# A decode block with its gradients: the first weight in longer rows, all slots in one tile, and one weight load cut by rows

## The chip, the cores and the metric

The kernel runs on one core of a Trainium2 chip. The metric is the device time of one execution in microseconds (us), as a median over runs.

## The reference

```python
def block(x, k_cache, v_cache, wq, wo, w1, w3, w2):      # cut from the reference
    q = (layernorm(x) @ wq)            # x: 4 x 1 x 512, wq: 512 x 4096, 32 heads of 128
    p = softmax(q . k_cache * Dh**-0.5)                  # k_cache, v_cache: 4 x 32 x 4096 x 128, bf16
    h = x + (p . v_cache) @ wo                           # wo: 4096 x 512
    return h + (silu(layernorm(h) @ w1) * (layernorm(h) @ w3)) @ w2    # w1, w3: 512 x 1792, w2: 1792 x 512

out, vjp = jax.vjp(block, x, k_cache, v_cache, wq, wo, w1, w3, w2)
return out, *vjp(grad_out)
```

There are 128 pairs of batch and head. Each has 1 MB of K and 1 MB of V to read, V is read a second time for the gradients, and 1 MB each of K's and V's gradient is written. The arithmetic per byte is small.

## The kernel before

On-chip memory is cut into 23 slots of 128 partitions x 8320 bytes, which are handed round by hand. K and V heads come in as 128 rows of 8192 bytes, one row to a partition, in the first half all on the sync engine's queue. The parts that the change touches (cuts marked):

```python
class Slot:
    def __init__(self, name, src=free):
        self.i = src.popleft()
        self.t = slotp.tile([P, SLOT], BF16, name=name, tag=f"slot{self.i}")   # one tile per slot
# ... cut
wq_s = [Slot(f"wq{cc}") for cc in range(DC)]
for cc in range(DC):                                     # first weight: 4 loads of 128 rows x 8192 bytes
    nc.sync.dma_start(out=wq_s[cc].b(HD), in_=A_wq[cc * P:(cc + 1) * P, :])
# ... cut: K loads follow, as far as slots are free
for h in range(H):
    for cc in range(DC):
        nc.tensor.matmul(qT_ps[:, h, :], lhsT=wq_s[cc].b(HD)[:, h * Dh:(h + 1) * Dh], rhs=xhatT[:, cc, :],
                         start=(cc == 0), stop=(cc == DC - 1))
# ... cut
def load_w2():                                           # down projection: 2 loads of 128 rows x 7168 bytes
    sl = two_slots("w2")
    for i in range(2):
        nc.sync.dma_start(out=sl[i].b(7 * D).rearrange("p (c j) -> p c j", c=7),
                          in_=B_w2.rearrange("(p c) j -> p c j", c=FC)[:, i * 7:(i + 1) * 7, :])
    return sl

def d_hh_units():                                        # w2 transposed, times grad_out: early in the first half
    w2 = load_w2()
    # ... cut
```

The first half (to about 700 us) streams K and V through scores, softmax and the V product. The second (from about 740 us) reads V again and writes both cache gradients.

## Time and profile before

| what | before | where it stands |
|---|---|---|
| time, median of 3 | 1722.01 us (1721.88 to 1723.07) | the runs |
| span of the profiled run | 1720.0 us | first line of the page |
| bytes moved | 707.86 MB, mean 412 GB/s | packet line |
| rate in 20 to 660 us | 411 to 419 GB/s at a DMA share of 1.01 | busy times by stretch |
| busiest compute engine | TensorE, 77% | busy times |

The DMA share says what part of the time the sixteen DMA engines had a packet in hand. GB/s says what they moved. A share of 1.01 says that they had one in hand all the time.

One more view is needed that is not on the page. The trace keeps each DMA packet's start, duration and size, and for each transfer the sixteen times at which its parts, one to a DMA engine, signalled completion. "Packets took ..." and "lag" below are read from these records; the lag of a transfer is the time from its first to its last part.

### The profile page before, as it was taken

The numbers are of one execution on the slowest core, as the hardware profiler recorded it, in microseconds if no ns is written. First come the engines' busy times: TensorE is split into PE (matmuls) and PEld (weight loads), VectorE is DVE, ScalarE is ACT, GpSimd is POOL, SyncE is SP. The second block draws the span as 40 slices with busy tenths as digits, with TensorE's granted clock in tenths as the row PEclk, the third lists the DMA queues.
The fourth block names the chain that finished last, engine by engine and source line by source line (L and its number), as shares of the span: only waits on it lengthen the run. The fifth ranks groups of instructions, "written<-read, shape, count | busy, mean of one in ns | idle before, by whom it ended". The sixth has DMA issues, their size and how long they took to land. (4 is left out here: it accounts for less than half of the span.)

```text
span 1720.0 us, 44172 instructions
## 1 busy us (share of the span) xinstructions
PE 1331.8 (77%) x19124; PEld 1131.8 (66%) x19124; DVE 1253.1 (73%) x1389; ACT 960.3 (56%) x1470; POOL 414.4 (24%) x689
## 2 busy tenths in 40 slices
PE   5889888888888888888788787883677778677852
PEld 4767766766667666877677777773565566555652
DVE  5989899899998997667676776763567557456575
ACT  3455444444454444677655555553676667676752
POOL 1211222222222231231322222321223122212220
PEclk8999999999999999666655555555875565565556
DMA  9999999999999999999999999999999999999996
GB/s 397 418 419 419 419 418 420 418 419 418 412 418 405 418 402 395 380 424 424 424 424 425 424 425 425 424 425 398 411 388 410 422 421 417 404 420 419 419 421 273
DMA packets 101762, 707.86 MB, mean 412 GB/s; under 512 B 11052, under 2 KB 15288, under 8 KB 17600
## 3 DMA queue, kind: packets, MB, share of 16 engines
q1 hardware_dynamic: 63568, 432.04, 60.9%
q0 software_dynamic: 20864, 148.22, 20.6%
q10 hardware_dynamic: 17136, 124.79, 17.7%
q8 instruction: 150, 2.46, 0.5%
q14 instruction: 44, 0.36, 0.1%
HBM read 422.59 MB, written 282.34 MB: 410 GB/s over the span
## 5 line engine op out<-in xcount | busy, mean ns | idle before, releaser
L761 ACT COPY V<-pt_tps 128x1024 bf16<-128x1024 bf16 x512 | 492.5, 1016 | 200.4 <-PE pt_tps L760 175.2
L760 PE MATMUL pt_tps<-ident_b,V 128*128 128x128 bf16 x4096 | 454.1, 293 | 82.9 <-ACT V L761 78.6
L760 PEld LDWEIGHTS <-V 128*128 128x128 bf16 x4096 | 402.7, 138 | 146.2 <-issue 137.1
L766 DVE TENSOR_TENSOR gv<-P,reps 128x4096 bf16<-128x4096 bf16 x125 | 287.2, 2297 | 195.8 <-ACT reps L1129 92.4
L766 DVE TENSOR_TENSOR gk<-dS,reps 128x4096 bf16<-128x4096 bf16 x128 | 294.0, 2297 | 113.5 <-DMA out_dram<-gv 90.8
L433 PE MATMUL M_ps<-PK,Vn 128*128 128x130 bf16 x4096 | 287.4, 223 | 46.4 <-DMA Vn<-in_A_v_cache_dram 44.3
L418 DVE TENSOR_TENSOR PK<-Kn,PK 128x4096 bf16<-128x4096 bf16 x128 | 292.3, 2284 | 31.7 <-POOL PK L414 31.4
L433 PEld LDWEIGHTS <-Vn 128*128 128x128 bf16 x4096 | 254.9, 100 | 67.1 <-DMA Vn<-in_A_v_cache_dram 59.2
L325 DVE STREAM_TRANSPOSE KT<-Kn 128x512 f32<-128x512 f32 (+1 forms) x321 | 250.6, 797 | 0.3 <-issue 0.2
L320 ACT COPY KT<-pt_tps 128x1024 bf16<-128x1024 bf16 x128 | 129.5, 1012 | 192.9 <-PE pt_tps L319 145.7
L777 POOL DMA_DIRECT2D out_dram<-gv x128 | 68.4, 534 | 673.2 <-DVE dSt L1158 581.9
L1148 PE MATMUL dP_ps<-dOT_bf,V 128*128 128x1 bf16 x4096 | 149.9, 166 | 83.4 <-ACT V L761 58.7
L1148 PEld LDWEIGHTS <-V 128*128 128x128 bf16 x4096 | 140.1, 103 | 96.8 <-ACT V L761 70.2
L1138 POOL COPY P<-P_all 128x64 bf16<-128x64 bf16 x125 | 157.8, 1263 | 0.0
L331 POOL TENSOR_TENSOR W<-qrep,wmask 128x128 bf16<-128x128 bf16 x128 | 123.6, 966 | 82.7 <-PE S_ps L351 67.8
L414 POOL COPY PK<-P_all 128x64 bf16<-128x64 bf16 x128 | 32.6, 255 | 421.4 <-ACT P_all L408 418.4
L408 ACT COPY P_all<-pt_P 32x64 bf16<-32x64 bf16 x256 | 52.1, 203 | 58.9 <-PE pt_P L404 56.7
L1129 ACT CAST reps<-rep_ps 128x512 bf16<-128x512 f32 x62 | 36.4, 587 | 83.8 <-PE rep_ps L1126 46.5
L319 PE MATMUL pt_tps<-ident_b,Kn 128*128 128x128 bf16 x1024 | 81.2, 224 | 0.0
L319 PEld LDWEIGHTS <-Kn 128*128 128x128 bf16 x1024 | 62.6, 100 | 25.8 <-issue 25.8
L443 PE MATMUL kP_ps<-PK,onesw 128*32 128x512 bf16 x1024 | 79.4, 387 | 0.0
L351 PE MATMUL S_ps<-KT,W 128*32 128x256 bf16 x1536 | 75.2, 285 | 0.5 <-DVE KT L325 0.2
(239 smaller groups left out, 1284.9 us busy)
## 6 DMA issues: line engine op xcount, KB each, us to landing
Kn<-in_A_k_cache_dram SPq DMA_DIRECT2D x128, 1024.0 KB, 15.7
Vn<-in_A_v_cache_dram SPq DMA_DIRECT2D x128, 1024.0 KB, 16.1
out_dram<-gv POOLq DMA_DIRECT2D x128, 1024.0 KB, 29.0
out_dram<-gk SPq DMA_DIRECT2D x128, 1024.0 KB, 22.7
V<-in_A_v_cache_dram ACTq DMA_DIRECT2D x119, 1024.0 KB, 15.1
V<-in_A_v_cache_dram SPq DMA_DIRECT2D x9, 1024.0 KB, 18.7
wq<-in_A_wq_dram SPq DMA_DIRECT2D x8, 1024.0 KB, 19.0
out_dram<-gw POOLq DMA_DIRECT2D x6, 896.0 KB, 38.3
```

Of the source, the lines that this page charges most:

```text
L319: nc.tensor.transpose(pt[:, i, :], Kn[:, c * GW + i, :], ident_b[:])
L320: nc.scalar.copy(out=KT[:, c * GW:(c + 1) * GW, :], in_=pt[:])
L325: nc.vector.transpose(out=KT[:, c * w_:(c + n) * w_], in_=Kn[:, c * w_:(c + n) * w_])
L331: nc.gpsimd.tensor_tensor(out=W[:, hl], in0=qrep[:, :, s:s + 1].to_broadcast([P, 4, 32]), in1=wmask[:, hl, None, :].to_broadcast([P, 4, 32 ...
L418: nc.vector.tensor_tensor(out=PK[:, :, 0:Dh].rearrange("p j (r t) -> p j r t", t=2), in0=Ks[s].heads().rearrange("p j (r t) -> p j r t", t=2),
L433: nc.tensor.matmul(hold["M"][:], lhsT=Vn[:, j, :], rhs=PK[:, j, :], start=(j == 0), stop=(j == SJ - 1))
L443: nc.tensor.matmul(hold["kP"][32 * q:32 * (q + 1), :, :], lhsT=ones_window(w), rhs=PK[:, j0:j0 + 4, 0:Dh], start=(w == 0 and c == 0), stop ...
L760: nc.tensor.transpose(pt[:, i, :], v[:, g * GW + i, :], ident_b[:])
L761: nc.scalar.copy(out=v[:, g * GW:(g + 1) * GW, :], in_=pt[:])
L766: nc.vector.tensor_tensor(out=dst.rearrange("p j (r t) -> p j r t", t=2), in0=col2[:, :, None, :].to_broadcast([P, SJ, Dh // 2, 2]), in1=r ...
L1138: nc.gpsimd.tensor_copy(out=P2s[s][:], in_=P_all[:, s, :, None].to_broadcast([P, SJ, 2]))
L1148: nc.tensor.matmul(dP_ps[:, j:j + 1], lhsT=VT[:, j, :], rhs=dOT_bf[:, s:s + 1], start=True, stop=True)
```

## The change

Its intent is threefold: to load the first weight in 16384-byte rows, two loads in place of four; to make every slot a slice of one tile, so that two neighbouring slots can take one such load; and to shift load off one DMA engine by cutting the down projection's weight, in the first half only, into 120 and 8 rows. The author's estimate of that shift: the cut spares one engine 16 rows of 7168 bytes and gives eight others two rows more each. At the 269 ns at which such rows start one after the other before, this is 16 x 269 ns = 4.3 us less on the one and 0.54 us more on each of the eight.

```diff
+    arena = slotp.tile([P, NSLOT * SLOT], BF16, name="arena")
     class Slot:
-            self.t = slotp.tile([P, SLOT], BF16, name=name, tag=f"slot{self.i}")
+            self.t = arena[:, self.i * SLOT:(self.i + 1) * SLOT]
 ... cut
-    for cc in range(DC):
-        nc.sync.dma_start(out=wq_s[cc].b(HD), in_=A_wq[cc * P:(cc + 1) * P, :])
+    wq_v = []
+    for a in range(0, DC, 2):
+        v = arena[:, wq_s[a].i * SLOT:wq_s[a].i * SLOT + 2 * HD].rearrange("p (c n) -> p c n", c=2)
+        nc.sync.dma_start(out=v, in_=A_wq[a * P:(a + 2) * P, :].rearrange("(p c) n -> p c n", c=2))
+        wq_v += [v[:, 0], v[:, 1]]
 ... cut: rows_to_T reads the activations with a stride of two, the q matmuls read wq_v[cc]
-    def load_w2():
+    def load_w2(cuts=(0, P)):
         sl = two_slots("w2")
         for i in range(2):
-            nc.sync.dma_start(out=sl[i].b(7 * D).rearrange("p (c j) -> p c j", c=7),
-                              in_=B_w2.rearrange("(p c) j -> p c j", c=FC)[:, i * 7:(i + 1) * 7, :])
+            for lo, hi in zip(cuts, cuts[1:]):
+                nc.sync.dma_start(out=sl[i].b(7 * D).rearrange("p (c j) -> p c j", c=7)[lo:hi],
+                                  in_=B_w2.rearrange("(p c) j -> p c j", c=FC)[lo:hi, i * 7:(i + 1) * 7, :])
 ... cut
     def d_hh_units():
-        w2 = load_w2()
+        w2 = load_w2((0, 120, P))
```

More of the change, by code (lines that the diff above doesn't have):

```diff
@@ L220, in rows_to_T @@
         pt = psA.tile([P, nchunks, n], FP32, tag="rT", name="pt_rT")
+        rows = src_rows.rearrange("b (a p c) -> b a c p", c=2, p=P)
         for c in range(nchunks):
-            nc.tensor.transpose(pt[:, c, :], src_rows[0:n, c * P:(c + 1) * P], ident_f[0:n, 0:n])
+            nc.tensor.transpose(pt[:, c, :], rows[0:n, c // 2, c % 2, :], ident_f[0:n, 0:n])
         nc.vector.tensor_copy(out=dst, in_=pt[:])
@@ L271 @@
             for cc in range(DC):
-                nc.tensor.matmul(qT_ps[:, h, :], lhsT=wq_s[cc].b(HD)[:, h * Dh:(h + 1) * Dh], rhs=xhatT[:, cc, :],
+                nc.tensor.matmul(qT_ps[:, h, :], lhsT=wq_v[cc][:, h * Dh:(h + 1) * Dh], rhs=xhatT[:, cc, :],
                                  start=(cc == 0), stop=(cc == DC - 1))
```

## The prediction

> **What bounds the kernel now.** I read the page's slices first, then the busy times by stretch, the first weight's own view, the last stretch, and last how the change moves instructions and waits on each engine.
>
> ```profile
> span 1720.0 us, 44172 instructions
> PE 1331.8 (77%) x19124; PEld 1131.8 (66%) x19124; DVE 1253.1 (73%) x1389; ACT 960.3 (56%) x1470; POOL 414.4 (24%) x689
> ...
> DMA  9999999999999999999999999999999999999996
> GB/s 397 418 419 419 419 418 420 418 419 418 412 418 405 418 402 395 380 424 424 424 424 425 424 425 425 424 425 398 411 388 410 422 421 417 404 420 419 419 421 273
> DMA packets 101762, 707.86 MB, mean 412 GB/s; under 512 B 11052, under 2 KB 15288, under 8 KB 17600
> ```
>
> No compute engine is above 77%, while the DMA row is full in 39 slices of 40 and the rate stands at 418 to 425 GB/s in most of them. 707.86 MB at 420 GB/s would be 1685 us: all but 35 us of the span is the transfer of bytes that the change leaves as they are. The stretches say where the 35 us are:
>
> ```profile
> 0.00:20.00 20.00, 7.26 (x165) 6.47 (x166) 6.36 (x24) 2.41 (x4) 3.86 (x21) 1.00 0.92 371
> 20.00:240.00 220.00, 187.44 (x3032) 153.00 (x3032) 196.44 (x268) 114.88 (x242) 50.72 (x131) 0.95 1.01 419
> 240.00:460.00 220.00, 185.71 (x3079) 151.93 (x3076) 202.33 (x267) 107.09 (x243) 57.15 (x128) 0.99 1.01 418
> 460.00:660.00 200.00, 166.27 (x2772) 137.90 (x2772) 182.28 (x243) 96.98 (x217) 54.96 (x119) 0.99 1.01 411
> 660.00:740.00 80.00, 70.12 (x1121) 60.50 (x1121) 51.07 (x77) 46.67 (x69) 16.07 (x21) 0.79 1.00 385
> 740.00:1190.00 450.00, 347.71 (x4376) 322.59 (x4374) 301.95 (x254) 256.94 (x284) 119.23 (x130) 0.56 1.01 425
> 1190.00:1320.00 130.00, 94.04 (x1340) 81.74 (x1341) 80.21 (x74) 87.85 (x102) 30.66 (x32) 0.74 0.98 394
> 1320.00:1690.00 370.00, 271.79 (x3216) 216.53 (x3214) 223.07 (x183) 245.77 (x313) 81.20 (x109) 0.58 1.01 418
> 1690.00:1720.00 30.00, 1.42 (x39) 1.16 (x35) 9.45 (x8) 1.69 (x2) 0.53 (x1) 0.55 0.51 211
> ```
>
> The last two columns are the DMA share and GB/s. From 20 to 660 us the share is 1.01[...]: no engine of the 16 lacks work. What is lost is lost in the first 20 us, around 660 to 740 and 1190 to 1320, and in the last 30. Of these the change touches only the first. Its weight:
>
> ```profile
> L132 SPq DMA_DIRECT2D wq<-in_A_wq_dram x4: 388/422/956, 0.7 to 2.1; - x4
> its engine sat idle before it (us, times) until:
>   DMA wq<-in_A_wq_dram: 7.1, 4
> ...
> DMA to landing us min/median/max: 5.3/8.4/11.4
> ```
>
> TensorE waits 7.1 us for the four loads and starts its last 125 matmuls at 13.57 us, but the DMA engines meanwhile fetch K and V, so this wait costs time only if they later run dry, and they do not before 460 us. The last stretch has a different cause:
>
> ```profile
> 1700.00:1705.00 5.00, 0.00 (x0) 0.00 (x0) 0.00 (x0) 0.00 (x0) 0.00 (x0) 0.50 0.87 362
> 1705.00:1710.00 5.00, 0.00 (x0) 0.00 (x0) 0.00 (x0) 0.00 (x0) 0.00 (x0) 0.50 0.07 31
> 1710.00:1715.00 5.00, 0.00 (x0) 0.00 (x0) 0.00 (x0) 0.00 (x0) 0.00 (x0) 0.50 0.07 28
> ```
>
> A share of 0.07 is one DMA engine of sixteen: one straggler works alone for some 12 us. The sixteen landing times of each transfer, which the trace holds, agree: fifteen parts of the last store are in by 1701.2 us, the sixteenth at 1717.5. The same landings give the lag between the first and the last engine earlier: 0.75 us after the first weight, 3.0 at 100 us, 9.3 at 450, 5.2 at 690. In the first half this lag is not one engine's. Eight of the sixteen each lose about 1.5 us in turn, at the times when a 16384-byte instruction fetch runs (150 of them, one per 10 us), and at 450 us these eight lie together, between 9.0 and 9.3 us behind.
>
> [...]
>
> **The change part by part.** First weight. A packet of 8192 bytes is recorded with 309 ns, one of 7168 with 272 and one of 3584 with 140 (medians); starts on one engine follow each other 3 ns sooner than these. 132 ns for 3584 bytes are 36.8 ns per KB, so 8192 bytes cost 295 of 306 ns and about 11 ns are the fixed part. Four loads of 128 rows are 32 packets on each engine; two loads of 16384-byte rows are 16. Saved: 16 x 11 = 0.18 us per engine, and two completion writes of about 6 ns. Sum: -0.19 us, an estimate. It is on the path as far as the engines are, from the first microsecond on.
>
> Wait order at the start. The sync engine keeps eight transfers in flight; with two loads fewer ahead, K runs two loads further forward (10 MB instead of 8 MB queued). With a share of 1.01 a deeper queue moves nothing: 0.
>
> Order of contraction. The rows are now interleaved in pairs, and the transposed activations are read with a stride of two; four small transposes (0.58 us together, at 8.9 us) and 128 matmuls of 166 ns in number, size and order as before: 0.
>
> Down projection's weight in the first half (about 60 us; the second load, at the end, stays uncut). [...] The sum over engines is zero, so the mean rate stays; only the lag changes. Two more issues on the sync queue (about 0.33 us each) cancel the two saved.
>
> One tile for all slots. Every engine keeps its instructions, shapes and order, apart from one small row that moves by a place. The waits change in few places: 65 of 1388 on VectorE, mostly a wait for ScalarE traded for another that has long been met; 2 of TensorE's go away with the two loads. One long wait goes: three small GpSimd copies that in before sat 26.4 us until 701 us for a V load now wait for GpSimd alone. Their reader, the first gradient product, starts at 706.0 us because of the row copied just before it, so the 26.4 us gain nothing: 0.
>
> Sum: -0.2 us, plus whatever the shifted lag does, between 0 and +0.5 us by the rivals below. 1722.0 - 0.2 + a little is 1721.9; I choose 1721.6, a little lower, because a tuner keeps a change rather when it gains.
>
> **The rivals.** First: [...] relieving it by 4.3 us brings the last K, V and weights in earlier, so that the phase ends up to 4 us sooner: 1718. For it: the author chose the cut, and from 460 us on the rate falls to 411[...]. Against it: at 450 us eight engines lie within 0.3 us of each other, so taking one out leaves seven in the same place.
>
> Second: [...] Then the last landing of the phase comes 0.5 us later: 1722.3. [...]
>
> Third: the new dependences of the one tile order something that ran freely, and a store or load of the second half is issued later. [...] a few microseconds, either way: 1718 to 1726. Against it: the waits compared above, which are nearly all met long before.
>
> Fourth: the first half ends sooner and the gain is swallowed at 700 to 740, where all engines drain (the lag falls to 0.4 us at 725 us) and the second half starts from a chain of small steps. Then even a correct gain of the first rival shows only in part.
>
> **Range and chances.** The three runs of before lie within 1.2 us. Mechanisms bring -4 to +0.5 us, a shifted schedule perhaps 2 us more: 1718.0 to 1724.5 for 8 in 10. Two per cent are 34 us. That is as much as all the time in which the engines are below their rate, so neither a gain nor a loss of that size has a source here: faster 0.01, same 0.98, slower 0.01.
>
> **What would show each step right or wrong.** First weight: its loads land together near 13.4 us, and packets of 16384 bytes take about 600 ns each, not less. The cut: after the 60 us mark the landings have one engine 4.3 us ahead of where it was, while the largest lag at 100 and 450 us stays at 3.0 and 9.3 (or 0.5 more if the second rival holds); if it falls by over 1 us, the first rival is right. Queue: share and GB/s of 20 to 660 us unchanged. One tile: GpSimd's wait of 26.4 us gone, the first gradient product still near 706 us. End: still a share of 0.07 for about 12 us, as the change does not touch the last stores. The prediction would be wrong if the tail's straggler vanished or grew by more than 5 us, or if VectorE or the sync queue showed a new wait of tens of microseconds.

## The result, and the profile after

| | before | after |
|---|---|---|
| time, median of 4 | 1722.41 us (1721.88 to 1723.07) | 1729.01 us (1727.73 to 1730.08) |
| ratio after to before | | 1.0038 (95%: 1.0020 to 1.0055) |
| span and clock of the profiled run | 1720.0 us, 0.749 | 1728.3 us, 0.761 |

Ratios here are the mean time of one kernel's fast runs over that of the other's in the same rounds, so not quite the ratio of the medians quoted. The change makes the kernel 6.6 us slower: "same" at the 2% mark, but outside the predicted range of 1718.0 to 1724.5.

Three lines of the page after: span, DMA share and rate in 40 slices of 43 us.

```profile
span 1728.3 us, 44122 instructions
...
DMA  9999999999999999999999999999999999999996
GB/s 397 366 418 418 419 418 419 417 416 418 414 414 411 418 403 391 378 422 423 424 425 424 425 425 425 424 425 402 394 393 405 425 419 415 404 418 422 420 421 271
```

The share is as full as before. Slice two of the rate, 43 to 86 us, reads 366 where before has 418; every other slice lies within 6 of its counterpart but one (394 for 411, near 1220 us). (418 - 366) x 43.2 us = 2.2 MB not moved, or 5.4 us at 418 GB/s. The same in two of the wide stretches that the prediction shows of before (columns: busy us and counts of TensorE, its weight loads, VectorE, ScalarE, GpSimd; granted clock, DMA share, GB/s):

```profile
20.00:240.00 220.00, 183.97 (x2947) 148.54 (x2946) 191.58 (x261) 113.31 (x236) 47.36 (x127) 0.95 1.01 408
240.00:460.00 220.00, 187.29 (x3080) 153.86 (x3080) 201.35 (x268) 105.64 (x241) 58.62 (x132) 0.98 1.01 417
```

408 against 419 GB/s in the first, at the same share of 1.01; 417 against 418 in the second. Within slice two, in steps of 4 us, before:

```profile
60.00:64.00 4.00, 4.00 (x80) 3.24 (x80) 3.82 (x4) 1.08 (x5) 1.57 (x2) 1.00 1.03 424
64.00:68.00 4.00, 2.81 (x38) 2.16 (x37) 3.75 (x11) 2.20 (x5) 1.11 (x5) 1.00 1.00 412
68.00:72.00 4.00, 3.33 (x56) 2.79 (x60) 3.33 (x3) 2.68 (x7) 0.24 (x1) 1.00 1.01 420
```

and after:

```profile
60.00:64.00 4.00, 3.79 (x78) 3.23 (x79) 3.83 (x3) 1.23 (x6) 1.27 (x2) 1.00 1.03 238
64.00:68.00 4.00, 3.12 (x43) 2.29 (x40) 3.69 (x9) 1.90 (x5) 1.39 (x5) 1.00 1.04 241
68.00:72.00 4.00, 0.04 (x1) 0.00 (x0) 3.61 (x4) 1.89 (x2) 0.00 (x0) 0.76 0.96 224
72.00:76.00 4.00, 0.94 (x9) 0.94 (x10) 0.00 (x0) 0.00 (x0) 0.00 (x0) 0.50 1.00 414
```

For 12 us all sixteen engines are busy (0.96 to 1.04) and move 224 to 241 GB/s instead of 412 to 424. Step by step that is 4 x (424 - 238)/424 + 4 x (412 - 241)/412 + 4 x (420 - 224)/420 = 5.3 us of transfer lost. It is the time in which the down projection's weight comes in: its 256 packets of 7168 bytes took 486 ns on average (median 480) where before they took 277 (274), and the 8192-byte packets of K and V sent between them took 570 ns against 313. At the end of the stretch TensorE runs dry, as its timeline after shows (start, duration, engine, work, in brackets the idle time before and what ended it):

```profile
75.06 2.51 PEld L438 LDWEIGHTS <-arena 128*128 128x128 bf16 x24 [7.10 <-DMA arena<-in_A_v_cache_dram]
```

It sat 7.10 us for a V load queued behind the slow one. How far the same VectorE instruction of the two traces is shifted tells when time was lost: 0.4 us until 67.8 us, 7.7 to 8.2 us from 72 to 100, 5.6 from 118 to 174, 4.4 to 7.1 until 660, 5.2 to 6.6 from 700 to 732, 5.7 to 7.6 from 750 to 1170, and 8.1 at the end of these two runs. The loss of 5.3 us in those 12 us is there at once, and it stays. The 1 to 3 us that come on top after 740 us are of these two profiled runs, and no run here explains them; the medians differ by 6.6 us.

The first weight's loads after, by their line (issue times, then from issue to landing), and the matmuls behind them:

```profile
L135 SPq DMA_DIRECT2D arena<-in_A_wq_dram x2: 392/406/421, 0.7 to 1.2; - x2
...
DMA to landing us min/median/max: 12.8/12.8/12.8
```

```profile
14.08 3.52 PE L277 MATMUL qT_ps<-xhatT,arena 128*128 128x4 bf16 x126 [3.23 <-DMA arena<-in_A_wq_dram]
```

They start at 14.08 us instead of 13.57. The end, in steps of 5 us after:

```profile
1713.30:1718.30 5.00, 0.00 (x0) 0.00 (x0) 0.00 (x0) 0.00 (x0) 0.00 (x0) 0.50 0.06 26
1718.30:1723.30 5.00, 0.00 (x0) 0.00 (x0) 0.00 (x0) 0.00 (x0) 0.00 (x0) 0.50 0.07 28
```

is what it was: one engine of sixteen, alone for about 12 us, only later.

### The profile page after: what moved, and what is told of

It reads as the page before. It is cut to its first block, busy times and chain, and to the rows that moved or that the text cites. A ratio compares the mean times of both kernels' runs of the same rounds, so it can differ in the third digit from the quotient of the medians.

```text
span 1728.3 us, 44122 instructions
## 1 busy us (share of the span) xinstructions
PE 1322.2 (77%) x19124; PEld 1122.8 (65%) x19124; DVE 1252.8 (72%) x1389; ACT 959.2 (56%) x1470; POOL 414.0 (24%) x689
## 3 DMA queue, kind: packets, MB, share of 16 engines
q0 software_dynamic: 20864, 148.22, 20.5%
## 5 line engine op out<-in xcount | busy, mean ns | idle before, releaser
L767 ACT COPY arena<-pt_tps 128x1024 bf16<-128x1024 bf16 x512 | 491.9, 1017 | 201.2 <-PE pt_tps L766 179.3
L766 PE MATMUL pt_tps<-ident_b,arena 128*128 128x128 bf16 x4096 | 445.6, 289 | 89.7 <-ACT arena L767 84.2
L766 PEld LDWEIGHTS <-arena 128*128 128x128 bf16 x4096 | 395.1, 136 | 153.4 <-issue 144.5
L772 DVE TENSOR_TENSOR arena<-P,arena 128x4096 bf16<-128x4096 bf16 x125 | 287.2, 2297 | 195.7 <-DMA out_dram<-arena 102.7
L772 DVE TENSOR_TENSOR arena<-dS,arena 128x4096 bf16<-128x4096 bf16 x128 | 294.0, 2297 | 113.3 <-DMA out_dram<-arena 101.0
L438 PE MATMUL M_ps<-arena 128*128 128x130 bf16 x4096 | 287.5, 223 | 64.9 <-DMA arena<-in_A_v_cache_dram 64.4
L423 DVE TENSOR_TENSOR arena<-arena 128x4096 bf16<-128x4096 bf16 x128 | 292.4, 2285 | 37.0 <-POOL arena L419 36.3
L438 PEld LDWEIGHTS <-arena 128*128 128x128 bf16 x4096 | 253.6, 99 | 86.9 <-DMA arena<-in_A_v_cache_dram 80.6
L330 DVE STREAM_TRANSPOSE arena<-arena 128x512 f32<-128x512 f32 (+1 forms) x321 | 250.5, 797 | 0.0
L325 ACT COPY arena<-pt_tps 128x1024 bf16<-128x1024 bf16 x128 | 129.4, 1012 | 196.0 <-PE pt_tps L324 153.1
L1154 PE MATMUL dP_ps<-dOT_bf,arena 128*128 128x1 bf16 x4096 | 149.8, 166 | 86.8 <-ACT arena L767 59.9
L1154 PEld LDWEIGHTS <-arena 128*128 128x128 bf16 x4096 | 139.0, 103 | 100.5 <-ACT arena L767 71.6
L324 PE MATMUL pt_tps<-ident_b,arena 128*128 128x128 bf16 x1024 | 80.2, 223 | 0.0
L448 PE MATMUL kP_ps<-arena,onesw 128*32 128x512 bf16 x1024 | 79.9, 389 | 0.0
L324 PEld LDWEIGHTS <-arena 128*128 128x128 bf16 x1024 | 61.7, 99 | 25.7 <-issue 25.6
```

Source lines behind the costliest of these rows:

```text
L324: nc.tensor.transpose(pt[:, i, :], Kn[:, c * GW + i, :], ident_b[:])
L325: nc.scalar.copy(out=KT[:, c * GW:(c + 1) * GW, :], in_=pt[:])
L330: nc.vector.transpose(out=KT[:, c * w_:(c + n) * w_], in_=Kn[:, c * w_:(c + n) * w_])
L423: nc.vector.tensor_tensor(out=PK[:, :, 0:Dh].rearrange("p j (r t) -> p j r t", t=2), in0=Ks[s].heads().rearrange("p j (r t) -> p j r t", t=2),
L438: nc.tensor.matmul(hold["M"][:], lhsT=Vn[:, j, :], rhs=PK[:, j, :], start=(j == 0), stop=(j == SJ - 1))
L448: nc.tensor.matmul(hold["kP"][32 * q:32 * (q + 1), :, :], lhsT=ones_window(w), rhs=PK[:, j0:j0 + 4, 0:Dh], start=(w == 0 and c == 0), stop ...
```

## The experiments

The theory after reading the two traces: the cut slows the packets themselves, its own (486 ns for 277) and those sent between them (570 for 313), because its pieces have fewer than 128 rows, with a price of its own for each shape. What in the shape would do that, no record of this case shows; the runs can ask only which shapes are slow.

The rivals: (A) it is the long rows or the one tile, not the cut; (B) it is the number of transfers or their smaller size; (C) any shape other than 128 rows is slow for itself, at one price for all of them; and the prediction's own first rival, that the relief of one engine matters.

### First round: which part, and is it rows or pieces

Four kernels, run on one chip beside seven runs of before (median 1721.86 us, 1721.41 to 1723.06).

**e1_no_cut**: the kernel after, with the weight uncut.

```diff
-        w2 = load_w2((0, 120, P))
+        w2 = load_w2()
```

> The whole change, but the down projection's weight in two loads of 128 rows again. All three theories that lay the loss on the cut ([...] fifteen: fifteen engines instead of sixteen; transfers: four transfers instead of two) expect the loss of 6.6 us to go almost whole: 1722.0 to 1723.5 us, and 418 GB/s again between 60 and 72 us. The theory that the one tile or the 16384-byte rows cost the time expects 1727 to 1729.

Measured 1723.57 us (1721.16 to 1725.18), ratio 1.0008 (0.9993 to 1.0023). The packets of 7168 bytes took 277 ns again, and the rate is back:

```profile
60.00:64.00 4.00, 3.94 (x80) 3.20 (x78) 3.84 (x4) 1.10 (x6) 1.63 (x2) 1.00 1.03 424
```

Rival A falls.

**e2_cut_only**: the kernel before, with the cut and nothing else.

```diff
-        w2 = load_w2()
+        w2 = load_w2((0, 120, P))       # load_w2 as in the change
```

> The kernel before, and only the cut into 120 and 8 rows. Theories of the cut: 1727 to 1729 us, with the packets of 7168 bytes at some 480 ns instead of 272. Theory of the one tile or the first weight: 1722 to 1723.

Measured 1728.64 us (1727.52 to 1729.47), ratio 1.0038 (1.0023 to 1.0053): the whole loss of the change, by the cut alone. The packets took 524 ns (median 522).

```profile
60.00:64.00 4.00, 4.00 (x80) 3.27 (x80) 3.81 (x4) 1.08 (x5) 1.56 (x2) 1.00 1.06 236
```

**e3_columns**: as many transfers, but each of 128 rows; the cut goes through the columns (4 and 3 of 7).

```diff
-                nc.sync.dma_start(out=sl[i].b(7 * D).rearrange("p (c j) -> p c j", c=7)[lo:hi],
-                                  in_=B_w2.rearrange("(p c) j -> p c j", c=FC)[lo:hi, i * 7:(i + 1) * 7, :])
+                nc.sync.dma_start(out=sl[i].b(7 * D).rearrange("p (c j) -> p c j", c=7)[:, lo:hi],
+                                  in_=B_w2.rearrange("(p c) j -> p c j", c=FC)[:, i * 7 + lo:i * 7 + hi, :])
-        w2 = load_w2((0, 120, P))
+        w2 = load_w2((0, 4, 7))
```

> The whole change, with the weight still in four transfers, but each of all 128 rows: columns are split (4096 and 3072 bytes a row). [...] Fifteen: no loss either. Transfers (four of them hold four of the eight places in the queue): still 1727 to 1729.

Measured 1722.64 us (1722.05 to 1723.53), ratio 1.0004 (0.9989 to 1.0019). Packets of 4096 bytes took 163 ns, of 3072 bytes 124 ns: 287 for what was 277 in one.

```profile
60.00:64.00 4.00, 3.60 (x75) 2.85 (x72) 3.80 (x4) 1.44 (x6) 1.97 (x4) 1.00 1.02 405
```

Rival B falls: four transfers cost nothing measurable, if each spans all rows.

**e4_64_64**: the cut in two equal halves, so that the sixteen engines have equal work and none is relieved (in e9 all sixteen signals of a 64-row load come with the data).

```diff
-        w2 = load_w2((0, 120, P))
+        w2 = load_w2((0, 64, P))
```

> The whole change, with the weight cut into 64 and 64 rows. Sixteen engines with four rows each, all the same work. [...] Fifteen: no loss, 1722 to 1723.5, since all sixteen engines work equally.

Measured 1729.03 us (1725.93 to 1731.52), ratio 1.0035 (1.0018 to 1.0051); packets took 576 ns (median 539).

```profile
60.00:64.00 4.00, 3.88 (x79) 3.32 (x80) 3.82 (x3) 1.15 (x6) 1.36 (x2) 1.00 1.01 158
```

An even split over all engines costs as much as the uneven one, so the loss is not an imbalance of work among engines. That leaves the shape of the pieces, with a price for each shape or with one price for all (rival C).

### Second round: size of the effect, the tail, and a miss

Four kernels beside seven runs of before (median 1722.59 us, 1720.33 to 1724.34).

**e5_one_tile**: the kernel before, with the slots as slices of one tile and nothing else.

```diff
+    arena = slotp.tile([P, NSLOT * SLOT], BF16, name="arena")
-            self.t = slotp.tile([P, SLOT], BF16, name=name, tag=f"slot{self.i}")
+            self.t = arena[:, self.i * SLOT:(self.i + 1) * SLOT]
```

> Only the one tile for all slots; the first weight in four loads and the down projection's weight in two, as before. If the cut is the whole loss, as the first four runs say: 1721.5 to 1723.5, same as before within 0.1%. If the one tile costs something that the first four runs hid behind the first weight's gain: above 1724.

Measured 1722.78 us (1720.57 to 1723.28), ratio 0.9997 (0.9982 to 1.0012). The one tile costs and brings nothing that can be seen.

**e6_k_120_8**: the same cut on other data, K's loads of heads 16 to 31, in the kernel before. If the cut itself is the cause, 16 MB must lose far more than 1.8 MB.

```diff
-            nc.sync.dma_start(out=Ks[s].heads(), in_=cache_head(A_k_cache, s))
+            cuts = (0, 120, P) if 16 <= s < 32 else (0, P)
+            for lo, hi in zip(cuts, cuts[1:]):
+                nc.sync.dma_start(out=Ks[s].heads()[lo:hi], in_=cache_head(A_k_cache, s)[lo:hi])
```

> The kernel before with sixteen of the 128 K loads (heads 16 to 31) cut into 120 and 8 rows: the cost of the cut many times over. [...] the cut weight (1.84 MB) cost 5 to 6 us, so sixteen loads of 1.05 MB each cost 46 to 52 us if all of it stays exposed[...]: 1755 to 1775 us. A theory that the loss came once, from a hole in the queue at that place, expects under 1735.

Measured 1789.59 us (1785.39 to 1794.18), ratio 1.0388 (1.0362 to 1.0413): 67 us slower, more than expected.

```profile
80.00:240.00 160.00, 99.51 (x1361) 83.02 (x1358) 82.86 (x112) 51.88 (x106) 15.10 (x54) 0.82 1.00 242
```

Share 1.00, 242 GB/s: against the 419 of before, 160 us x (1 - 242/419) = 67.6 us, the whole difference. The count seems to have left out that V's loads in the same queue, of 128 rows as ever, are slowed too: in steps of 20 us from 80 to 220 us, 8192-byte packets of both together took 479 to 596 ns on average (315 before), and if only K's half had doubled to 612 the mean would be about 460. What passes the delay on to loads of 128 rows, no run shows by itself.

**e7_112_16**: the cut at 112 rows. Both pieces have parts on all sixteen engines: in e9, for 112 rows and for 16, all sixteen signals come with the data.

```diff
-        w2 = load_w2()
+        w2 = load_w2((0, 112, P))
```

> The kernel before with the weight cut into 112 and 16 rows. Both parts use all sixteen engines, with seven rows and one. [...] A theory that any shape other than 128 rows is slow for itself expects about 500 ns and 1727 to 1729 again.

Measured 1727.03 us (1726.37 to 1729.38), ratio 1.0026 (1.0011 to 1.0041), packets 504 ns (median 492). The author's own estimate was lower than that of rival C and did not hold.

```profile
60.00:64.00 4.00, 3.79 (x78) 3.06 (x75) 3.82 (x4) 1.25 (x6) 1.79 (x2) 1.00 1.04 212
```

504 ns and 1727.03 us are what rival C expects: about 500 ns, 1727 to 1729 us. But packets here run among those of K and V; what a shape costs by itself had to be tested without the stream: e9 below.

**e8_gv_sync**: a look at the tail and its straggler. V's gradient stores, which before has on GpSimd and so on the software queue (q0 of its page, 148.22 MB), go out through the sync engine.

```diff
-        nc.gpsimd.dma_start(out=rows_of(out_3[b, h]), in_=gv.heads())
+        nc.sync.dma_start(out=rows_of(out_3[b, h]), in_=gv.heads())
```

> Not a test of the cut but of its aim. The kernel before with the V gradient's stores issued by the sync engine instead of GpSimd. If the one engine that works alone for the last 12 us is slow because of the software queue, its lag goes and the end comes up to 12 us earlier: 1708 to 1716. If it is slow for another reason: 1720 to 1726. If the sync engine's eight places in flight are too few for loads and all stores: slower, 1730 or more.

Measured 1724.23 us (1721.87 to 1728.46), ratio 1.0003 (0.9986 to 1.002). The end of its trace still has one or two engines working on while the others are done, for some 6 us at shares of 0.14, 0.12 and 0.09 in steps of 2 us, where before has one for 12 us. The lag of V's gradient stores that land after 1700 us falls from between 18 and 25 us to 10, but that of K's rises from between 5 and 8 us to between 9 and 10. So the software queue has a part in the straggle, but moving these stores off it neither removes the stragglers nor gains time.

### Third round: the shapes by themselves, and a try at the tail

Two kernels beside fourteen runs of before (median 1721.53 us, 1719.54 to 1723.47).

**e9_probe**: e5's kernel with twelve loads ahead of everything, two of each shape, each alone (it waits for the one before) and each of about 1 MB in packets of 8192 bytes. Only the number of rows differs; with fewer rows a row is made of more packets. The total time means nothing.

```diff
+    def probe(n):                       # n rows into slots that are free at the start
+        s = P // n if P % n == 0 else 1
+        # ... cut: out = arena[0:n, s slots of 4096], in = rows of one K head
+    for rep in range(2):
+        for n in (128, 120, 112, 64, 32, 16):       # written out in the kernel
+            o, i = probe(n)
+            nc.sync.dma_start(out=o, in_=i)
```

> The disputed cost by itself. With one tile for all slots, twelve extra loads of 0.92 to 1.05 MB go ahead of the first weight, each alone (each waits for the one before): 128, 120, 112, 64, 32 and 16 rows, twice; where there are fewer rows, each is a multiple of 8192 bytes, written as packets of 8192. [...] Any other shape than 128 rows slow for itself: about 306 ns once and 500 to 550 ns five times, 16 rows no worse than 64. Neither (only in traffic): 306 ns six times. The time of the whole is 60 to 100 us more than before and means nothing.

| rows | measured us from issue to landing | packet ns, mean of the first and the second load |
|---|---|---|
| 128 | 4.9 to 5.1 | 365, 397 |
| 120 | 6.9 to 7.0 | 572, 568 |
| 112 | 5.5 to 5.7 | 494, 478 |
| 64 | 7.5 to 7.6 | 612, 605 |
| 32 | 7.7 to 7.8 | 611, 604 |
| 16 | 12.1 | 1076 |

Four of the six shapes as the trace answers for them, in the order 128, 112, 64 and 16 rows (duration of the issue, when issued; then issue to landing):

```profile
L139 SPq DMA_DIRECT2D arena<-in_A_k_cache_dram x2: 365/377/389, 0.7 to 45.9; - x2
...
DMA to landing us min/median/max: 4.9/5.0/5.1
...
L143 SPq DMA_DIRECT2D arena<-in_A_k_cache_dram x2: 317/317/317, 12.7 to 57.8; - x2
...
DMA to landing us min/median/max: 5.5/5.6/5.7
...
L145 SPq DMA_DIRECT2D arena<-in_A_k_cache_dram x2: 571/620/669, 18.4 to 63.4; - x2
...
DMA to landing us min/median/max: 7.5/7.5/7.6
...
L149 SPq DMA_DIRECT2D arena<-in_A_k_cache_dram x2: 560/565/570, 33.8 to 78.6; - x2
...
DMA to landing us min/median/max: 12.1/12.1/12.1
```

The means hold slow first packets. Without the first sixteen of each load they are 313 ns for 128 rows, 539 to 543 for 120, 420 to 444 for 112, 585 to 595 for 64, 587 to 601 for 32, and 1116 for 16 (first load only: the second's packets mix with the next load's).

The number of engines does not explain this. Of the sixteen signals of a 120-row load one comes 0.5 us after the issue and fifteen after 6.1 to 7.0 us, as if one engine had no part in it; for every other shape all sixteen come with the data. Rival C, one price for every other shape, falls: sixteen rows take 12.1 us for the same megabyte as sixty-four in 7.5, and 112 rows take only 0.6 us more than 128. 64 and 32 rows are alike (7.5 to 7.6 and 7.7 to 7.8 us), though one has twice the rows of the other. So the price is one for each shape, but it does not simply follow the number of rows: 120 rows (6.9 to 7.0 us) are slower than 112 (5.5 to 5.7). The packets of 112 rows, at 420 to 444 ns without the first ones, take 34 to 42% longer than 313, and those of e7 took 504 ns for 277, or 82% longer; why the stream adds to it is not shown.

One rival was not named: another shape may also change which addresses of the main memory are read together. No run separates reading from writing, and the traces don't tell which rows an engine gets.

**e10_last_stores**: can the same cut help where only one engine works anyway? In the kernel before, the last three stores of K's gradient are cut into 120 and 8 rows, which takes eight rows of each from one engine (in e9 one of the sixteen signals of a 120-row load comes 0.5 us after the issue, fifteen after 6.1 to 7.0). If that engine is the straggler, it is spared 24 packets of 306 ns, 7.3 us of work, and the estimate is 1714 to 1719 us.

```diff
-            nc.sync.dma_start(out=rows_of(out_2[b, h]), in_=gk.heads())
+            cuts = (0, 120, P) if s >= NH - 3 else (0, P)
+            for lo, hi in zip(cuts, cuts[1:]):
+                nc.sync.dma_start(out=rows_of(out_2[b, h])[lo:hi], in_=gk.heads()[lo:hi])
```

> The aim of the cut, at the place where the profile shows one engine working alone: the kernel before with the last three K gradient stores in 120 and 8 rows. Fifteen engines are idle there for 12 us, so the cut's own cost should hardly show. [...] If it is another engine, nothing is gained and the cut costs something: 1722 to 1728.

Measured 1724.93 us (1723.13 to 1726.97, 11 runs), ratio 1.0020 (1.0011 to 1.0029): slower by 3.4 us.

```profile
1705.00:1710.00 5.00, 0.00 (x0) 0.00 (x0) 0.00 (x0) 0.00 (x0) 0.00 (x0) 0.50 0.68 239
1710.00:1715.00 5.00, 0.00 (x0) 0.00 (x0) 0.00 (x0) 0.00 (x0) 0.00 (x0) 0.50 0.15 56
```

The lone stretch is shorter, but the last of the other fifteen now lands some 8 us later (about 1714 us, before 1706) and the straggler 2.7 us later (1720.2, before 1717.5). Stores that read the on-chip memory in this shape pay too: from 1695 to 1705 us the rate is 295 to 297 GB/s at shares of 0.95 to 0.97. No version was found that beats the kernel before. Which of the sixteen is the straggler, and why it alone is late, stays open.

## Why the prediction was wrong, by its own steps

**The bound.** Right, and it is why the loss shows in full: with the engines at a share of 1.01 from 20 to 660 us, 5.3 us of transfer lost at 60 to 72 us are 4.4 to 7.1 us of delay from 118 to 660. The prediction's argument that no time could be lost there, because no engine lacks work, was the trap: a share of 1.03 goes with 424 GB/s before and with 238 after.

**The cut: the step that failed.** In the prediction's words, "The sum over engines is zero, so the mean rate stays; only the lag changes." It priced each row of the cut loads at the 269 ns that rows take in a load of 128. The split of the rows fits: in after's trace each of the two 120-row loads (issued at 47.80 and 50.06 us) has one signal 0.5 us after its issue and fifteen with the data, each 8-row load has eight with the data, and after the cut one engine leads the next. But that the lead is 4.06 us at 95 us, predicted 4.3, is partly luck: 16 rows spared at 486 ns would be 7.8 us, and the lead was 7.3 us at 75 us before it shrank (6.3 and then 2.99 in e2). The price of a row was wrong: 486 ns instead of 277 on average, and 570 instead of 313 for K and V packets sent meanwhile. The 269 ns came from before's trace, where the weight comes in as loads of 128 rows; the price of a row in a load of 120 was not shown there. This term was to be zero and is +5.3 us; e2 shows that it is all of the change (+6.8 us by medians), e1 that nothing remains without it. The prediction asked how many rows each engine gets, and not whether a row keeps its price in the new shape. That the shape is the cause rests on e3 and e4 (277 ns in one piece, 287 in two of 128 rows, 576 in halves) and on e6 and e9; what in it slows the packets is not shown, as no record names the engines or the rows that each of them gets.

**First rival, relief of one engine.** Refuted. The lead of 4 us is gone by 440 us, where the foremost engine leads the next by only 0.15 us (0.08 in e2), and the largest lag there is 9.65 us after, 9.47 in e2, 9.29 in e1, 9.31 before. Its sign, that the rate falls to 411 from 460 us on, was weak: the share there is 1.01, so hardly any engine was without a packet, and at least part of the lower rate is that 8192-byte packets took 319 ns on average where they took 316 earlier. Seven others stood in the same place, as the prediction held against it, and e4, which relieves nobody, takes the same time. The prediction's sign for 100 us failed: the largest lag there was to stay at 3.0 us and is 6.6 (5.3 in e2, 3.6 in e1), since the relieved engine ran ahead and was not one of those behind.

**Second rival, half a microsecond more on eight engines.** Whether the eight that get two rows more are the eight that lie behind, no trace tells. Not settled: the largest lag at 440 us is 0.16 to 0.37 us longer in the two cut kernels than in the two uncut, in one trace each. Against 5.3 us it doesn't matter.

**Third and fourth rival.** Neither happened. No new wait cost time, e5 takes the time of before, and what was lost at 60 us passed the standstill of 700 to 740 us nearly whole (5.2 us).

**First weight, -0.19 us.** Too large by any reading. A 16384-byte packet starts 608 ns after the one before, a pair of 8192-byte ones takes 2 x 306 = 612: 4 ns saved per pair, not 11, so 16 x 4 = 0.06 us. The 11 ns is a slip in the sum: 132 ns for 3584 bytes are 36.8 ns per 1000 bytes, and 8192 bytes are 8.19 of these, not 8, so they cost 302 of the 306 ns and the prediction's own figures give 4. (They don't bear much: 140 ns is the shortest of the 3584-byte packets, whose median is 144. What the prediction calls completion writes are packets of 4 bytes: 6608 on the sync engine's queue before, sixteen to each of its 413 transfers, of 9 ns in the median.) And the first packets of the start mostly took 1.2 to 2.2 us each, against 0.8 to 1.3. The matmuls start at 13.69 (e1), 13.77 (e3) and 14.08 us (after) with the new loads, at 13.57 (before), 13.40 (e2) and 13.27 (e5) with the old. "Near 13.4" did not come; the loss of some tenths is not resolved in the times.

**Queue, order of contraction, one tile.** Right within what can be measured (e1, e5). In before's trace at most eight of the sync engine's 413 transfers are between issue and landing at once, as the prediction has it. GpSimd's 26.4 us wait for the V load went (its next instruction now waits 28.0 us, for VectorE, in its place), and the first gradient product starts at 711.27 us against 706.04: later by just the 5.2 us that everything is shifted by.

**The end.** Right: one engine alone for some 12 us, unchanged.

**The range.** It held no case in which the engines stay busy and move less. Every rival asked where work waits; none asked whether a new shape of transfer keeps the speed of the old. That rival, with twice the packet time for 1.8 MB (1.84 MB / 420 GB/s = 4.4 us), would have stood at 1726 and belonged in the range.

## What to carry to other kernels

Cut a transfer by columns, not by rows, if it must be cut: four pieces of 128 rows cost nothing measurable (e3, ratio 1.0004), while two pieces of 120 and 8 rows (e2, 216 to 236 GB/s from 60 to 72 us, where before has 412 to 424) or of 64 and 64 rows (e4, 158 to 220 GB/s there) about halved the rate for as long as they ran, and 8192-byte packets of other transfers sent meanwhile took 570 ns for 313 (after). Before pricing a transfer of a new shape, time that shape, by itself as in e9 (a megabyte in 4.9 to 5.1 us to 128 rows, 6.9 to 7.0 to 120, 12.1 to 16) and in the stream as in e2; a duration from the old shape is no price for it. And read GB/s beside the DMA share: here twelve microseconds at shares of 0.96 to 1.04 ran at 224 to 241 GB/s.
